# Two-way attention and a rational feed-forward layer on one core: batch 0's attention by token halves, the first weights joined in halves, and a new order of work

## The chip, the cores and the metric

One core of a Trainium2 chip runs the whole kernel in one launch. The metric is the device time in microseconds. A profile records one execution of the program; its span goes from the first to the last instruction.

## The reference

```python
def _attn_ref(x, state):                     # x: 8 x 8 x 512 x 64, state: 8 x 8 x 32 x 64
    scores = scale * np.matmul(x, state.transpose(0, 1, 3, 2))
    scores = scores - scores.max(-1, keepdims=True)
    a = np.exp(scores)
    a /= a.sum(-1, keepdims=True) + 1e-09
    xread = np.matmul(a, state)
    scores2 = scale * np.matmul(state, x.transpose(0, 1, 3, 2))
    ...
    sread = np.matmul(a2, x)
    return np.concatenate([xread, sread], axis=2)

def _moe_ref(x, w_in, w_out, a, b):          # 4608 x 512, 512 x 2048, 2048 x 512
    h = x @ w_in
    P = a[0] + a[1] * h + a[2] * h2 + a[3] * h3
    Q = 1.0 + np.abs(b[0]) * np.abs(h) + np.abs(b[1]) * h2
    g = P / (Q + 1e-06)
    return g @ w_out
```

Tokens read from 32 state slots per head and slots read from 512 tokens per head. The 544 rows of each of 8 batches then go through a layer whose activation is a ratio of two polynomials. The weights arrive as 64-bit numbers.

## The kernel before

**The work.** A unit of work is a pair of a batch `b` and one of eight slices `u` of the 2048 hidden columns, n = 8b + u; 64 units for the tokens, and 8 more (n = 64 to 71) for the slots of all batches together. Instead of `xread` times `w_in` the kernel multiplies the state by the slice of `w_in` first (`extra`, L689, token `X`, 32 small matmuls at L695, for two batches at a time), and the attention weights with that product afterwards (`front`, L762, token `F`, at L785). Both are split in a high and a low float32r part, so each `F` has 6 matmuls, two `F` per unit. The products for later batches go to DRAM (`xs`, L716) and come back (`lm`, L735).

**One unit.** `FC` and `FB` (ScalarE, L794, L801) and `mu`, `po`, `qd` (VectorE, L806, L810, L816) form the polynomials from the PSUM tile `h`; `qa`, `ln`, `ex` (ScalarE, L822, L891, L902) the reciprocal; `g1`, `g2`, `g3` (VectorE, L826, L833, L839) the high part `gh` and the rest; `gl` (GpSimd, L845) the low part; `mh` (4 matmuls) and `ml` (2 matmuls, both at L857) add the product with `w_out` for one 128-token block `t`.

**The weights.** Each slice of `w_in` and `w_out` is a group `g` of raw 64-bit words, 128 x 1024 of them, loaded in two halves of 512 KB (`lr`, L271). `cp` (ScalarE, L293) takes the upper words of one half, `jr` (VectorE, L308) the lower words of the whole group, `jl` (VectorE, L313) joins both to float32. Group 0 is slice 0 of `w_in`, which the first `X` needs. `wh` and `wl` split a `w_out` slice.

**Batch 0's attention** has functions of its own (L507 to L605). `scores0` (L507) takes half of the tokens, from `xT` loads of 512 KB, into two PSUM banks, one for even and one for odd heads (parity `j`). Everything after goes by parity: `sc_copy0` copies one bank (ScalarE), `row_T0` transposes it (TensorE, L528), `row_max0`, `row_sub0` (VectorE), `row_exp0` (ScalarE), `row_sum0` (VectorE) and `row_norm0` (GpSimd) are the softmax over slots; `a_T0` transposes back, `a_hi0` and `a_lo0` (L585, L590) write the two parts of `aT`. `col_max`, `col_scale`, `col_exp` are the softmax over tokens, `e2_T0` and `e2_copy0` its transposes, and `sread` (L607) with `sr_copy`, `sr_T`, `sr_fin` the read by the slots.

**What sets the order.** `ORDER` (L23 to L195) is a string of tokens, one per call, with the arguments behind colons. The program walks it, and each engine executes its own instructions in that order; semaphores are added where one needs another's result. SP issues nearly all DMAs in that order too, so a DMA that waits for a buffer holds up those behind it. The PSUM tiles `h`, `ps_x`, `ps_c`, `ps_sr` share two slots of two banks (tag `h`); the other four banks (tags `o0` to `o3`) hold the output sums, and at the start batch 0's small tiles. The raw weights, and later `lm`, share two buffers, but for groups that borrow the place of a later `wo`. `lc`, `cb`, `cv` load, spread and copy the constants; `b0a` the absolute value of one. `lx` loads the next tile of `xT` or `x` in the order in which the list uses them; `ls` loads the state, `ws` stores a joined slice, `lw` loads it again, `os` stores output.

Of the kernel before, what the change touches and what calls it, by code (L numbers as in the profile page):

```python
# [1028 lines left out]
```

## Time and profile before

| | us |
|---|---|
| median of 3 runs | 674.07 |
| lowest and highest | 673.9, 674.11 |
| the profiled execution, its own time | 675.09 |
| its span | 673.3 |

The profiled execution took 1.79 us more than its span, and 1.02 us more than the median. In the views each engine has its name: PE is TensorE, PEld its weight loads, DVE VectorE, ACT ScalarE, POOL GpSimd, SP the queue that issues DMAs. A `q` behind the name is the engine's sequencer. An arrow in a wait points from the one that waits to the one waited for. Names of tiles stand as out<-in.

### The profile page before, as it was taken

How to read it: one execution, taken by the hardware profiler on the slowest of the kernel's cores; microseconds unless marked ns; L12 is line 12 of the kernel's file. 1: busy time of each engine (PE TensorE's matmuls, PEld its weight loads, DVE VectorE, ACT ScalarE, POOL GpSimd, SP SyncE). 2: the span in 40 equal slices, each digit the busy share in tenths (PEclk: the TensorE clock that was granted, in tenths of full speed). 3: DMA queues.
4: the chain of work that ended last, by engine and by line, in shares of the span. 5: the costliest groups of instructions: out<-in, count | busy, mean ns of one | idle time of the engine just before them, and what ended most of it. 6: DMA issues, size and time to landing. Idle time of an engine off the chain costs nothing.

```text
span 673.3 us, 11301 instructions
## 1 busy us (share of the span) xinstructions
PE 650.9 (97%) x4474; PEld 509.5 (76%) x4474; DVE 629.3 (93%) x583; ACT 521.7 (77%) x633; POOL 307.8 (46%) x174
## 2 busy tenths in 40 slices
PE   4699999999999999999999999999999999999997
PEld 2466667877877777878878878778778788788895
DVE  4999999899999898999999999999999999998886
ACT  4989989887978788878687777877786868777473
POOL 0234446534644545363544355443554444544540
PEclk9979999999999999999999999999999999999999
DMA  8979887343066164044232210412220311203301
GB/s 329 373 253 356 297 285 251 110 142 127 17 180 210 48 215 149 29 134 140 85 107 88 91 48 17 139 49 77 95 79 17 125 33 47 64 31 94 91 21 47
DMA packets 30679, 85.67 MB, mean 127 GB/s; under 512 B 3490, under 2 KB 3618, under 8 KB 30626
## 3 DMA queue, kind: packets, MB, share of 16 engines
q1 hardware_dynamic: 30290, 84.56, 36.9%
q8 instruction: 35, 0.57, 0.4%
q10 hardware_dynamic: 336, 0.39, 0.3%
q14 instruction: 18, 0.15, 0.1%
HBM read 57.15 MB, written 27.79 MB: 126 GB/s over the span
## 4 chain that ended last, share of the span: by engine, by line
PE 41%; DVE 34%; ACT 11%; issue 9%; POOL 2%; DMA 1%; SPq 0%; DVEq 0%; POOLq 0%; ACTq 0%
PE h L785 13%; DVE gh L829 7%; DVE C L808 5%; DVE A L818 5%; DVE A L835 5%; DVE C L812 3%; DVE C L841 3%; PE ps_x L695 2%; POOL gl L848 2%; PE o__5821 L857 2%; PE o__5809 L857 2%; ACT A L824 1%; ACT cv_y L300 1%; ACT C L797 1%; DVE aT L500 1%
## 5 line engine op out<-in xcount | busy, mean ns | idle before, releaser
L848 POOL TENSOR_TENSOR gl<-C,L 128x1024 fp32r<-128x1024 f32 (+1 forms) x70 | 176.0, 2516 | 255.1 <-DVE C L841 164.9
L785 PE MATMUL h<-aT,m 128*128 128x512 f32 x768 | 188.8, 392 | 1.3 <-DVE m L731 0.6
L785 PEld LDWEIGHTS h<-aT,m 128*128 128x128 f32 x768 | 142.5, 188 | 37.2 <-DVE m L731 2.3
L829 DVE SCALAR_TENSOR_TENSOR gh<-C,cst,L 128x1024 fp32r<-128x1024 f32 (+1 forms) x72 | 94.4, 1312 | 12.9 <-ACT L L904 9.9
L797 ACT ACTIVATE C<-h,cst 128x1024 f32<-128x1024 f32 (+1 forms) x72 | 83.3, 1157 | 28.1 <-PE h L785 23.2
L804 ACT ACTIVATE A<-h,cst 128x1024 f32<-128x1024 f32 (+1 forms) x72 | 76.8, 1067 | 32.6 <-PE h L785 26.9
L744 POOL TENSOR_TENSOR m<-m_sb,m 128x512 fp32r<-128x512 f32 x56 | 80.1, 1439 | 36.2 <-ACT m L740 20.4
L835 DVE SCALAR_TENSOR_TENSOR A<-A,gh 128x1024 f32<-128x1024 f32 (+1 forms) x72 | 91.5, 1270 | 1.7
L841 DVE SCALAR_TENSOR_TENSOR C<-C,cst,A 128x1024 f32<-128x1024 f32 (+1 forms) x72 | 89.4, 1246 | 1.4
L824 ACT ACTIVATE A<-A 128x1024 f32<-128x1024 f32 (+1 forms) x72 | 72.9, 1013 | 22.9 <-DVE A L818 22.5
L818 DVE SCALAR_TENSOR_TENSOR A<-A,b0a,h 128x1024 f32<-128x1024 f32 (+1 forms) x72 | 86.9, 1215 | 3.4 <-ACT A L804 2.4
L812 DVE SCALAR_TENSOR_TENSOR C<-C,cst,h 128x1024 f32<-128x1024 f32 (+1 forms) x72 | 87.7, 1219 | 1.9
L808 DVE TENSOR_TENSOR C<-C,h 128x1024 f32<-128x1024 f32 (+1 forms) x72 | 82.9, 1152 | 4.2 <-ACT C L797 3.8
L894 ACT ACTIVATE L<-A 128x1024 f32<-128x1024 f32 (+1 forms) x72 | 73.0, 1014 | 5.2 <-POOL gl L848 1.4
L904 ACT ACTIVATE L<-L 128x1024 f32<-128x1024 f32 (+1 forms) x72 | 72.9, 1013 | 1.8
L695 PE MATMUL ps_x<-win_sb,st 64*32 64x256 f32 x1024 | 37.7, 420 | 2.9 <-DVE win_sb L320 2.2
L740 ACT CAST m<-m_sb 128x512 fp32r<-128x512 f32 x56 | 34.0, 615 | 5.1 <-PE h L785 2.2
L695 PEld LDWEIGHTS ps_x<-win_sb,st 64*32 64x32 f32 x1024 | 18.1, 114 | 18.1 <-issue 7.4
L337 POOL TENSOR_TENSOR wo<-cv_r,wo 128x512 fp32r<-128x512 f32 x16 | 21.7, 1378 | 19.6 <-ACT wo L330 19.6
L785 PEld LDWEIGHTS h<-sh,m 128*128 128x128 f32 x192 | 23.9, 191 | 1.6 <-POOL sh L912 0.6
L785 PE MATMUL h<-sh,m 128*128 128x256 f32 x192 | 24.4, 284 | 0.4 <-POOL sh L912 0.4
L490 POOL TENSOR_TENSOR e<-e,rs 128x512 f32<-128x512 f32 x14 | 16.4, 1189 | 17.6 <-DVE rs L484 13.1
(246 smaller groups left out, 1109.1 us busy)
## 6 DMA issues: line engine op xcount, KB each, us to landing
m_sb<-m_dram SPq DMA_DIRECT2D x56, 256.0 KB, 3.0
xT_sb<-in_xT_dram SPq DMA_DIRECT2D x16, 512.0 KB, 4.4
x_sb<-in_x_dram SPq DMA_DIRECT2D x16, 512.0 KB, 6.9
m_dram<-xo SPq DMA_DIRECT2D x16, 512.0 KB, 4.2
win_sb<-w_in_dram SPq DMA_DIRECT2D x16, 512.0 KB, 5.0
out_dram<-o_sb SPq DMA_DIRECT2D x32, 256.0 KB, 3.7
raw<-in_w_in_dram SPq DMA_DIRECT2D x10, 512.0 KB, 7.5
raw_w<-in_w_out_dram SPq DMA_DIRECT2D x8, 512.0 KB, 7.2
```

Source lines behind the costliest of these rows:

```text
L744: nc.gpsimd.tensor_tensor(m[:, 1], MF.pop(n), m[:, 0].bitcast(F32), op=ALU.subtract)
L785: nc.tensor.matmul(h[:, ci * W : (ci + 1) * W], l, r, start=(q == 0), stop=(q == len(seq) - 1),)
L797: nc.scalar.activation(e["C"], e["h"], AF.Identity, scale=cst[:, 3:4], bias=cst[:, 2:3])
L804: nc.scalar.activation(e["A"], e["h"], AF.Abs, scale=cst[:, 5:6])
L808: nc.vector.tensor_tensor(e["C"], e["C"], e["h"], op=ALU.mult)
L812: nc.vector.scalar_tensor_tensor(e["C"], e["C"], cst[:, 1:2], e["h"], op0=ALU.add, op1=ALU.mult)
L818: nc.vector.scalar_tensor_tensor(e["A"], e["A"], b0a, e["h"], op0=ALU.add, op1=ALU.mult)
L824: nc.scalar.activation(e["A"], e["A"], AF.Abs)
L829: nc.vector.scalar_tensor_tensor(e["gh"], e["C"], cst[:, 0:1], e["L"], op0=ALU.add, op1=ALU.mult)
L835: nc.vector.scalar_tensor_tensor(e["A"], e["A"], 1.0 + 1e-6, e["gh"].bitcast(F32), op0=ALU.add, op1=ALU.mult)
L841: nc.vector.scalar_tensor_tensor(e["C"], e["C"], cst[:, 0:1], e["A"], op0=ALU.add, op1=ALU.subtract)
L848: eng.tensor_tensor(e["gl"], e["C"], e["L"], op=ALU.mult)
```

## The change

Batch 0's scores go into the shared two-bank PSUM tile, and the steps from `sc_copy0` to `a_lo0` take half of the tokens with both parities instead of one parity with all tokens. `scores0` now calls `scores` (L373), which is the same but for the place. `jr` and `jl` take a half as a second argument; without one they work on the whole group as before. `cp`, `front` and `mm` get a form that takes a whole group, or half a unit (numbers from 100 on); no token of the new list uses these forms. The list has the same tokens as before, but for `jr:0` and `jl:0`, which become `jr:0:0`, `jr:0:1`, `jl:0:0` and `jl:0:1`, in another order from the first on; both lists end with `ml:71:0 fl:71:0 os:71:0 ml:70:1 ml:71:1 fv:71:1 os:71:1`. Shown up to `F:2:0`:

```diff
 ORDER = [
-    "lx ls:0:2 lc pre lx scores0:0 scores0:1 sc_copy0:0 sc_copy0:1 row_T0:1 col_max:0 row_T0:0 lr:0:0 "
-    "cp:0:0 lr:0:1 jr:0 cp:0:1 row_max0:0 lr:1:0 ls:2:8 cp:1:0 jl:0 X:1 row_max0:1 row_sub0:1 "
-    "row_exp0:1 X:0 row_sub0:0 row_exp0:0 XA:1 lr:1:1 cp:1:1 lr:3:0 jr:1 X:2 row_sum0:0 row_norm0:0 "
-    "col_scale:0 col_exp:0:0 e2_T0:0 XA:0 fh:0 row_sum0:1 col_exp:0:1 lr:2:0 fo:0 XA:2 a_T0:0 a_hi0:0 "
-    "row_norm0:1 jl:1 a_T0:1 lr:2:1 a_hi0:1 cb cv X:4 lr:4:0 lr:4:1 cp:2:0 cp:2:1 a_lo0:0 lr:3:1 XA:4 "
-    "a_lo0:1 F:0:0 jr:2 F:0:1 jl:2 fh:1 cp:3:0 fo:1 F:1:0 lx F:1:1 lx cp:4:0 b0a jr:3 col_eps:0 "
-    "cp:3:1 jr:4 FB:0 FC:0 jl:3 wh:3 wl:3:0 lr:5:0 wl:3:1 lr:5:1 FB:1 qd:0 qa:0 ln:0 ex:0 mu:0 qd:1 "
-    "po:0 ws:1 e2_T0:1 e2_copy0:0 e2_copy0:1 sread:0:0 sread:0:1 cp:5:0 jr:5 cp:5:1 FC:1 g1:0 qa:1 "
-    "mh:0:2 xs:1 g2:0 col_norm:0 sr_copy:0 g3:0 xs:0 lr:7:0 lr:7:1 ln:1 sr_T:0 sr_fin:0 cp:4:1 ws:0 "
-    "ex:1 mu:1 po:1 X:5 XA:5 gl:0 jl:5 wh:5 wl:5:0 jl:4 lr:8:0 g1:1 X:8 XA:8 fh:2 cp:7:0 cp:7:1 "
-    "mh:0:0 ml:0:0 fo:2 lr:6:0 lr:6:1 xs:5 jr:7 lr:9:0 xs:2 X:9 lr:8:1 g2:1 xs:4 jl:7 wl:5:1 XA:9 "
-    "F:2:0 F:2:1 FC:2 FB:2 X:6 cp:6:0 lr:11:0 g3:1 lr:9:1 mh:0:1 jr:6 XA:6 xs:6 ml:0:1 qd:2 cp:6:1 "
...
+    "ls:0:2 pre lx scores0:0 sc_copy0:0 lr:0:0 cp:0:0 row_T0:0 jr:0:0 jl:0:0 row_max0:0 row_sub0:0 lx "
+    "scores0:1 sc_copy0:1 row_T0:1 row_exp0:0 lr:0:1 cp:0:1 jr:0:1 ls:2:8 col_max:0 jl:0:1 "
+    "col_scale:0 col_exp:0:0 col_exp:0:1 row_max0:1 row_sub0:1 row_exp0:1 row_sum0:0 row_norm0:0 X:1 "
+    "row_sum0:1 lr:1:0 cp:1:0 lr:1:1 jr:1 X:0 XA:1 XA:0 fh:0 fo:0 cp:1:1 jl:1 X:2 a_T0:0 XA:2 lc cb "
+    "cv a_hi0:0 a_lo0:0 row_norm0:1 a_T0:1 a_hi0:1 a_lo0:1 e2_T0:1 lr:2:0 cp:2:0 lr:2:1 b0a jr:2 "
+    "cp:2:1 jl:2 X:4 fh:1 XA:4 lr:4:0 cp:4:0 lr:3:0 cp:3:0 lr:3:1 lr:4:1 cp:3:1 F:0:0 F:0:1 FB:0 fo:1 "
+    "col_eps:0 col_norm:0 F:1:0 F:1:1 lr:5:0 jr:3 jl:3 xs:1 jr:4 FC:0 wh:3 wl:3:0 wl:3:1 FB:1 qd:0 "
+    "qa:0 e2_T0:0 ln:0 ex:0 e2_copy0:0 e2_copy0:1 mu:0 qd:1 cp:5:0 po:0 lr:5:1 jr:5 cp:5:1 xs:0 lx lx "
+    "sread:0:0 g1:0 mh:0:2 ws:0 cp:4:1 qa:1 FC:1 lr:7:0 xs:4 g2:0 sread:0:1 sr_copy:0 mh:0:3 jl:5 "
+    "wh:5 sr_T:0 sr_fin:0 g3:0 ln:1 ex:1 ws:1 mu:1 po:1 lr:7:1 X:5 XA:5 X:8 XA:8 gl:0 ml:0:2 jl:4 "
+    "g1:1 fh:2 lr:6:0 fo:2 cp:7:0 jr:7 cp:6:0 mh:0:1 cp:7:1 lr:6:1 cp:6:1 X:9 F:2:0 g2:1 xs:2 xs:5 "
...
 ]
@@ -291,12 +290,12 @@
             )
 
     def conv_parts(g, k):
-        if k == 0:
+        if k != 1:
             y = cv.tile([P, 4 * CW], I32, name="cv_y", tag="cv")
             r = cv.tile([P, 4 * CW], I32, name="cv_r", tag="cv")
             CV[g] = y, r
         y = CV[g][0]
-        sl = slice(2 * k * CW, (2 * k + 2) * CW)
+        sl = slice(0, 4 * CW) if k == 2 else slice(2 * k * CW, (2 * k + 2) * CW)
         nc.scalar.activation(
             y[:, sl].bitcast(F32),
             RAW[g][:, sl, 1].bitcast(F32),
@@ -305,20 +304,36 @@
             alpha=-(2.0**32),
         )
 
-    def join_rest(g):
+    def words(k):
+        return slice(0, 4 * CW) if k is None else slice(2 * k * CW, (2 * k + 2) * CW)
+
+    def join_rest(g, k=None):
+        sl = words(k)
         nc.vector.tensor_scalar(
-            CV[g][1], RAW[g][:, :, 0], 2.0**-29, 7.0, op0=ALU.mult, op1=ALU.min
-        )
-
-    def join(g):
+            CV[g][1][:, sl],
+            RAW[g][:, sl, 0],
+            2.0**-29,
+            7.0,
+            op0=ALU.mult,
+            op1=ALU.min,
+        )
+
+    def join(g, k=None):
         what, u = groups[g]
         y, r = CV[g]
         w = r
         if what == "in":
-            w = win_t[u] = ld.tile([P, NP, CW], F32, name="win_sb", tag="win", bufs=3)
-            w = w.rearrange("p c f -> p (c f)").bitcast(I32)
+            if not k:
+                win_t[u] = ld.tile([P, NP, CW], F32, name="win_sb", tag="win", bufs=3)
+            w = win_t[u].rearrange("p c f -> p (c f)").bitcast(I32)
+        sl = words(k)
         nc.vector.scalar_tensor_tensor(
-            w, y, 3, r, op0=ALU.logical_shift_left, op1=ALU.bitwise_or
+            w[:, sl],
+            y[:, sl],
+            3,
+            r[:, sl],
+            op0=ALU.logical_shift_left,
+            op1=ALU.bitwise_or,
         )
 
     def store_win(u):
@@ -505,25 +520,16 @@
         return ps_o.tile([P, S], F32, name=name, tag=f"o{t}")
 
     def scores0(g):
-        xt = X.pop(("xT", 0, g))
+        scores(0, g)
+
+    def tokens_of(t, g):
+        return t[:, :, g * (S // 2) : (g + 1) * (S // 2)]
+
+    def sc_copy0(g):
+        T = TS[0]
         if g == 0:
-            TS[0] = {"pj": [obank("ps_sc0", j) for j in range(2)]}
-        w = S // 2
-        for k in range(NP):
-            for j in range(2):
-                nc.tensor.matmul(
-                    TS[0]["pj"][j][k * NS : (k + 1) * NS, g * w : (g + 1) * w],
-                    st[j * D : (j + 1) * D, 0, k, :],
-                    xt[j * D : (j + 1) * D, k, :],
-                    start=True,
-                    stop=True,
-                )
-
-    def sc_copy0(j):
-        T = TS[0]
-        if j == 0:
             T["s"] = at.tile([P, 2, S], F32, name="sT", tag="sT")
-        nc.scalar.copy(T["s"][:, j], T["pj"][j])
+        nc.scalar.copy(tokens_of(T["s"], g), tokens_of(T["ps"], g))
 
     def transposes0(ps, src):
         for t in range(NT):
@@ -531,10 +537,17 @@
                 ps[:, t * P : (t + 1) * P], src[:, t * P : (t + 1) * P], ident
             )
 
-    def row_T0(j):
+    def row_T0(g):
         T = TS[0]
-        T["pr", j] = obank("ps_s0", 2 + j)
-        transposes0(T["pr", j], T["s"][:, j])
+        T["pr", g] = obank("ps_s0", 2 + g)
+        s = tokens_of(T["s"], g)
+        for t in range(NT):
+            j, i = divmod(t, NT // 2)
+            nc.tensor.transpose(
+                T["pr", g][:, t * P : (t + 1) * P],
+                s[:, j, i * P : (i + 1) * P],
+                ident,
+            )
 
     def half(t):
         return t.rearrange("p (a s) -> p a s", s=NS)
```

The parts of `front`, `mm` and `mm_hi` that the list doesn't use are left out here.

## Rows read from the trace of the kernel before

**Rows 1.** The page, part 1: busy us, share of the span, instructions.

```profile
PE 650.9 (97%) x4474; PEld 509.5 (76%) x4474; DVE 629.3 (93%) x583; ACT 521.7 (77%) x633; POOL 307.8 (46%) x174
```

**Rows 2.** Windows: stretch, length, busy PE, PEld, DVE, ACT, POOL, granted clock, DMA share, GB/s.

```profile
14.00:33.00 19.00, 13.94 (x166) 8.92 (x154) 17.58 (x27) 18.64 (x31) 4.60 (x4) 0.99 0.99 390
33.00:45.00 12.00, 11.33 (x172) 6.60 (x173) 11.24 (x11) 10.71 (x17) 5.03 (x3) 0.59 0.62 192
45.00:160.00 115.00, 113.81 (x1041) 83.00 (x1041) 109.50 (x104) 102.21 (x124) 55.38 (x31) 1.00 0.68 235
160.00:640.00 480.00, 477.65 (x2886) 383.51 (x2886) 460.50 (x404) 367.57 (x429) 233.38 (x124) 1.00 0.28 90
...
42.00:43.00 1.00, 1.00 (x3) 0.77 (x4) 0.49 (x1) 1.00 (x3) 0.75 (x1) 0.63 0.91 365
```

**Rows 3.** Waits of TensorE, whole span: us in total, times, longest.

```profile
PE ps_sr L618 <- ACT e2T L605: 4.8, 1, 4.8
PE ps_x L695 <- DVE win_sb L320: 2.2, 2, 1.9
...
PE o__4169 L857 <- POOL gl L848: 0.4, 1, 0.4
```

**Rows 4.** Timeline of TensorE, 0 to 46 us: start, us, engine, line, operation.

```profile
5.17 1.11 PE L514 MATMUL ps_sc<-xT_sb,st 64*32 64x256 f32 x16 [5.17 <-DMA xT_sb<-in_xT_dram]
6.72 1.11 PE L514 MATMUL ps_sc<-xT_sb,st 64*32 64x256 f32 x16 [0.44 <-DMA xT_sb<-in_xT_dram]
...
12.99 5.44 PE L695 MATMUL ps_x<-win_sb,st 64*32 64x256 f32 x96 [1.92 <-DVE win_sb L320]
...
20.66 1.10 PE L695 MATMUL ps_x<-win_sb,st 64*32 64x256 f32 x32 [0.24 <-DVE win_sb L320]
21.68 6.00 PE L785 MATMUL h<-aT,m 128*128 128x512 f32 x24
27.52 0.60 PE L530 MATMUL ps_e<-ident,e 128*128 128x128 f32 x4
32.95 2.21 PE L618 MATMUL ps_sr<-x_sb,e2T 128*32 128x64 f32 x64 [4.83 <-ACT e2T L605]
35.09 2.08 PE L857 MATMUL o__409<-wo,gh 128*128 128x512 f32 x4
...
38.15 3.67 PE L695 MATMUL ps_x<-win_sb,st 64*32 64x256 f32 x64 [0.62 <-ACT srT L641]
...
44.81 1.43 PE L785 MATMUL h<-aT,m 128*128 128x512 f32 x5
```

**Rows 5.** Timeline of ScalarE, 0 to 46 us.

```profile
7.92 1.07 ACT L526 COPY sT<-ps_sc 128x512 f32<-128x512 f32 x2 [5.46 <-PE ps_sc L514]
...
14.29 1.23 ACT L566 ACTIVATE e<-e 128x512 f32<-128x512 f32 x2 [2.79 <-DVE e L560]
...
25.11 1.15 ACT L804 ACTIVATE A<-h,cst 128x1024 f32<-128x1024 f32 x1
...
32.33 1.05 ACT L605 COPY e2T<-ps_e 128x512 f32<-128x512 f32 x2
```

**Rows 6.** Timeline of VectorE, 0 to 46 us.

```profile
9.02 1.22 DVE L398 TENSOR_REDUCE cm<-sT 128x2 f32<-128x1024 f32 x1 [9.02 <-ACT sT L526]
...
11.72 1.22 DVE L320 SCALAR_TENSOR_TENSOR win_sb<-cv_y,cv_r 128x1024 int32<-128x1024 int32 x1
...
41.22 1.27 DVE L829 SCALAR_TENSOR_TENSOR gh<-C,cst,L 128x1024 fp32r<-128x1024 f32 x1
```

**Rows 7.** VectorE by line and shape: count, busy us, mean ns, idle before.

```profile
L808 DVE TENSOR_TENSOR C<-C,h 128x1024 f32<-128x1024 f32 x64 | 77.5, 1211 | 2.0 <-ACT C L797 1.6 <-issue 0.4
...
L731 DVE TENSOR_TENSOR m<-ps_x,m 128x512 fp32r<-128x512 f32 x8 | 5.5, 682 | 1.1 <-ACT m L727 1.1
```

**Rows 8.** The tile `x_sb`, 10 to 40 us: from issue to landing.

```profile
DMA to landing us min/median/max: 11.1/11.3/11.5
```

**Rows 9.** The page, part 5: the group of `gl`.

```profile
L848 POOL TENSOR_TENSOR gl<-C,L 128x1024 fp32r<-128x1024 f32 (+1 forms) x70 | 176.0, 2516 | 255.1 <-DVE C L841 164.9
```

More of the change, by code (lines that the diff above doesn't have):

```diff
@@ L583, in a_T0, with by_parity @@
         transposes0(T["pa", j], T["e1"][:, j])
+    def by_parity(t):
+        return t.rearrange("p (j t) -> p j t", j=2)
     def a_hi0(j):
@@ L587, in a_hi0 @@
             AT[0] = at.tile([P, 2, 2, S], F32R, name="aT", tag="aT", bufs=2)
-        nc.scalar.copy(AT[0][:, 0, j], TS[0]["pa", j])
+        nc.scalar.copy(tokens_of(AT[0][:, 0], j), by_parity(TS[0]["pa", j]))
     def a_lo0(j):
@@ L592, in a_lo0 @@
         nc.vector.tensor_tensor(
-            a[:, 1, j], TS[0]["pa", j], a[:, 0, j].bitcast(F32), op=ALU.subtract
+            tokens_of(a[:, 1], j),
+            by_parity(TS[0]["pa", j]),
+            tokens_of(a[:, 0], j).bitcast(F32),
+            op=ALU.subtract,
         )
@@ L760, in attention_rational_ffn, with unit, of_half @@
     EW, SRS, O, OS = {}, {}, {}, {}
-    def front(n, ci):
-        b = n // U
-        if b < B:
+    HALVES = 100
+    def unit(n):
+        return n if n < HALVES else (n - HALVES) // 2
+    def of_half(n):
+        return None if n < HALVES else (n - HALVES) % 2
+    def front(n, ci):
+        half = of_half(n)
+        b = unit(n) // U
+        if half is not None:
+            W = S // 2
+            cols = slice(half * W, (half + 1) * W)
+            rhs = [(AT[b][:, 0, j, cols], AT[b][:, 1, j, cols]) for j in range(2)]
+        elif b < B:
             rhs = [(AT[b][:, 0, j, :], AT[b][:, 1, j, :]) for j in range(2)]
@@ L770, in front @@
             W = B * NS
-        if ci == 0:
+        if ci == 0 and half != 1:
             h = ps_h.tile([P, 2, S], F32, name="h", tag="h")
-            h = h.rearrange("p f w -> p (f w)")[:, : 2 * W]
-            EW[n] = {"h": h, "W": W, "N": 2 * W}
+            EW[n] = {"h": h.rearrange("p f w -> p (f w)")[:, : 2 * W], "W": W, "N": 2 * W}
+            if half == 0:
+                EW[n + 1] = {"h": h[:, 1], "W": W, "N": 2 * W}
         h = EW[n]["h"]
         hh, hl, lh = [], [], []
-        for (m, g), (rh, rl) in zip(M[n], rhs):
+        for (m, g), (rh, rl) in zip(M[unit(n)], rhs):
             mh = m[:, 0, g, ci * P : (ci + 1) * P]
@@ L850, in mm @@
     def mm(n, t, parts):
-        u = n % U
+        u = unit(n) % U
         e = EW[n]
         W = e["W"]
+        x = t * P % W
         for j in range(2):
@@ L858, in mm @@
                     O[t],
-                    e[l][:, j * W + t * P : j * W + (t + 1) * P],
+                    e[l][:, j * W + x : j * W + x + P],
                     WO[u][:, j, k, :],
@@ L865, in mm_hi @@
     def mm_hi(n, t):
-        if n % U == 0:
+        if unit(n) % U == 0:
             O[t] = ps_o.tile([P, DM], F32, name=f"o{t}_", tag=f"o{t}")
```

318 rows, old and new, of the table ORDER are left out of this document.

## Prediction, made before the changed kernel ran

> **What bounds the kernel now.** I read the page first, then the windows, TensorE's waits, and the first 46 us of the timeline one engine at a time.
>
> The page shows TensorE (PE) busy 650.9 of 673.3 us [rows 1]. The windows say where the rest lies: from 45 to 640 us it idles 1.19 and then 2.35 us, so 19 of the 22.4 idle microseconds lie in the first 45 us and in the tail [rows 2]. In that middle VectorE (DVE) is busy too, 109.5 of 115 us and then 460.5 of 480. So the steady part is bound by TensorE with VectorE right behind it, and a change can earn only what the start loses, plus what waits are left in the middle.
>
> TensorE's list of waits puts its two largest waits on another engine into the start: 4.8 us for the copies of `e2T` on ScalarE (ACT) and 2.2 us for the first joined weights [rows 3]. On its timeline [rows 4] the scores begin at 5.17, the first `X` (L695) at 12.99, the first `F` (L785) at 21.68, `sread` at 32.95 after a hole since 28.1, and the next `F` at 44.81. The engine also runs slowly there: 96 matmuls of L695 take 5.44 us from 12.99, 57 ns each, and 32 of them 1.10 us from 20.66, 34 ns each; 64 of them take 3.67 us from 38.15. The granted clock of 33 to 45 us is 0.59, a mixture of the two levels 1.2 and 2.4 GHz [rows 2]. The mean of 14 to 33 us is 0.99 and that of 42 to 43 us 0.63 [rows 2], so the clock fell at the end of the hole and rose again near 42.7.
>
> ScalarE stands 2.79 us waiting for VectorE's subtraction up to 14.29, and from there to the copies at 32.33 it is filled without a gap worth the name [rows 5] (18.64 of 19 us from 14 to 33 [rows 2]). So the hole ends when ScalarE has worked through its queue, and that queue starts when VectorE has finished the first softmax steps.
>
> **Part one: halves at the start.** The first half of group 0's weights now stands in the DMA queue between the two halves of `xT`, and 512 KB take 1.55 us there (the two scores start at 5.17 and 6.72 [rows 4]). So the first scores start as before, the second ones one transfer later, at about 8.3. Scores 1.1 and a copy of half of 1.07 [rows 5] bring the second `sc_copy0` to 9.95. On VectorE `col_max:0` (1.22 [rows 6]) follows to 11.15, then only the second half of the join, about 0.65, instead of the 1.22 at 11.72 behind a `row_max0`. The first half of `jr`, `jl`, `row_max0` and `row_sub0` fits in ahead of 9.95, where VectorE was idle until 9.02. `X:1` starts at 11.9, 1.1 us earlier than 12.99.
>
> Splitting costs something: a 128x512 operation takes 682 ns where a 128x1024 one takes 1211 [rows 7], so two halves cost 0.15 us more each for `jr` and `jl`. The first halves are hidden under the wait for `xT`; without that cover it would be 0.3 us. The copies in token halves read two pieces of 256 instead of one of 512; no row has that shape, I bound it by 0 and 0.1 us each and take 0.
>
> **Part two: ScalarE's queue.** Its steady stretch starts at 12.0 (`col_exp`, which needs `col_scale` at 11.9) instead of 14.29, with as much left to do: one `row_exp0` is done already, `cp:1:0` is not yet. Before, that work took 25.11-14.29 = 10.8 us, up to `FB:0` [rows 5]. That would give 22.8. But `X:1`, `X:0` and `X:2` still run at 57 ns a matmul, 1.8 us each, so `XA:2` waits for `X:2` until 17.3, `cv` for the spread of the constants until 18.5, and `fh:1` for `X:4` until 20.7: 0.95 us in all. `FB:0` starts at 23.75, 1.35 us earlier (bounds: 2.3 without those waits, 0 if they grow to that size). From `FB:0` to `e2_copy0` the same eight steps follow, 32.33-25.11 = 7.2 us [rows 5], so `sread:0:0` starts at 31.6 instead of 32.95.
>
> Its `x` tiles are now issued behind `xs:1`, `lr:5:1` and `xs:0` in SP's queue; `lr:5:0` ahead of them waits for `jr:1` and `cp:1:1`, until 17. They took 11.1 to 11.5 us from issue to landing [rows 8]; issued at 18 to 19 they land by 30. If that cover is gone, each microsecond past 31.6 costs one, for `mh:0:2` and all else on TensorE stand behind it.
>
> **Part three: from sread to the second F.** Before, 11.86 us lie between 32.95 and 44.81, almost all at the low level: `sread` 2.21, `mh:0:2` 2.08, 64 of `X` 3.67 [rows 4]. Now `sread` is cut in two and `mh:0:2`, `mh:0:3` are put between, so that TensorE has hardly a hole from 31.6 to 38. ScalarE and VectorE set bounds to the gain. On VectorE `jr:4` ends at 25.9; `qd`, `mu`, `qd`, `po` at 1.24 each, `jr:5` 0.65 and `g1:0` 1.27 [rows 6] end at 32.8, and `g2`, `jl:5`, `g3`, `mu:1`, `po:1` at 39.0. On ScalarE the copies end at 31.9; three `cp` of 0.6, `qa` 1.1, `FC` 1.2, `sr_copy` 0.5, `wh:5` 0.95 and `sr_fin` 0.3 end at 37.75. If the clock stays up or returns by about 36, TensorE meets these bounds: `X:5` starts at 37.8, `X:8` behind `po:1` at 39.05; `ln:1`, `ex:1`, `XA:5`, `XA:8`, `fh:2` end at 41.7, `fo:2` (0.7) at 42.4, and `F:2` starts at 42.6. If it stays low until 42.7 as before, the two halves of `sread` (1.1 each) and two `mh` (2.08 each [rows 4]) end at 38.05, for `g1:0` holds the first `mh` until 32.85; `sr_T` and `sr_fin` take until 38.95, both `X` 3.67 to 42.6, then `ml`, `mh` and `X:9` 2.5, and `F:2` starts at 45.2. I take 43.4, nearer to the early end: before, the rise near 42.7 came after TensorE had run almost unbroken since 38.15, and now the unbroken stretch begins at 31.6. Ahead of `F:2` one `mh` more is done than before, four matmuls, 0.9 us at the high level. TensorE's lead is 44.81-43.4+0.9 = 2.3 us.
>
> The Trainium skill ("TensorE: Matmul & The Clock Gate", HAM oscillation) says that a long idle pause throttles the array again, so that the next burst starts cold. The trace agrees, with its fall in the hole that ends at 32.95; by that rule alone the new hole, from 27.3 to 31.6, brings the fall back, and the sum would be that of the second rival.
>
> **Part four: the rest of the list.** All later work is the same in another order. What it can win is bounded by the idle time of TensorE from 45 to 640 us, 3.5 us [rows 2]; I bound the loss by as much and take 0. Both lists end with the same seven tokens.
>
> **Sum.** The profiled execution took 675.09 us for its span of 673.3. Less 2.3 that is 672.8. The median of the runs is 674.07, 1.02 lower, which gives 671.8.
>
> **The rivals.**
> - *The clock does not fall at all.* For: the hole is 0.5 us shorter. Against: it is still 4.3 us long. Then `F:2` starts at 42.6, the lead is 3.1 and the time 671.0.
> - *The clock stays low as long as before.* For: the hole. `F:2` at 45.2 with 0.9 us of work done ahead is a lead of 0.5: 673.6.
> - *VectorE takes the lead away.* `g1:1` starts at 41.22 [rows 6]; now it comes behind `po:1` and `jl:4`, at 40.2, only 1.0 us earlier, for `jr:4` stands ahead of `qd:0` in the new order. With 109.5 of 115 us busy, VectorE can give back only some of TensorE's lead. Then 1.0 us remains: 673.1. Against it: TensorE's idle share of the middle is smaller than VectorE's. The Trainium skill ("Perfetto Trace Analysis", Identifying the Most-Contended Engine) says that matmul busy time is no good measure and weight loads are the better one; those are busy 76% here, under VectorE's 93% [rows 1]. By that, this rival would be the likeliest; the trace cannot decide it.
> - *Slower: the new list meets GpSimd's products late.* An output matmul stands in order on TensorE, and a `gl` (L848) takes 2.5 us, 70 times [rows 9]; before, the longest wait on one in the middle is 0.4 us [rows 3]. If the new order has `ml` ahead of its `gl` four times by 1 us in the 600 us, 4.0 us are lost against 2.3 won: 675.8. It decides from 2.3 us of such waits on.
>
> **How the numbers follow.** About 0.2% (1.35 us) is what a measurement of this kernel can tell from no change, so faster means below 672.7. Forecast 0.40 (own range 670.8 to 673.0, 0.37 of it faster), clock stays up 0.15 (faster), clock low as long 0.17 (same), VectorE 0.16 (0.04 faster, 0.12 same), slower 0.12. That makes faster 0.37+0.15+0.04, and 0.02 for a middle that gains by itself, 0.58; same 0.30; slower 0.12. The range goes from 669.7 (the fast rival with a good microsecond of the middle's waits gone) to 674.8, which leaves out most of the slower case.
>
> **What would show it.** In the profile after: first `X` (L695) at 11.9, first `F` (L785) at 20.7 instead of 21.68, first `FB` (L804 before) at 23.75, `sread` at 31.6, a granted clock of 33 to 45 us above 0.59, `F:2` near 43.4; and from 45 us on TensorE idling no more than 3.5 us up to 640. A first `X` at 13 or later would say that the third transfer or the split join is late; a `sread` that waits for a DMA would say that the `x` tiles were the price; waits of `o` for `gl` above 2 us in sum would speak for the slower rival.

## The result, and the profile after

The changed kernel takes **664.14 us** (median of four runs, 663.78 to 664.94) against 673.99 for the kernel before, run beside it: ratio 0.9858 [0.9841, 0.9875], 9.9 us less. The forecast was 671.8 with a range of 669.7 to 674.8, so the direction was right and the size was not: 7.7 us of the gain were not foreseen. The profiled execution took 664.94 us with a span of 663.1, 10.15 us under the one of before.

Of the page after: busy time of each engine, as in [rows 1], and of part 4 (the chain that ended last) the shares by engine.

```profile
PE 643.5 (97%) x4474; PEld 508.5 (77%) x4474; DVE 624.8 (94%) x585; ACT 521.5 (79%) x633; POOL 313.5 (47%) x174
...
PE 87%; DVE 6%; issue 3%; DMA 2%; ACT 2%; POOL 0%; SPq 0%; DVEq 0%; POOLq 0%; ACTq 0%
```

The same line of part 4 for the kernel before:

```profile
PE 41%; DVE 34%; ACT 11%; issue 9%; POOL 2%; DMA 1%; SPq 0%; DVEq 0%; POOLq 0%; ACTq 0%
```

TensorE is busy 97% of the span in both, and VectorE 93 and 94%. By these shares nothing has changed. The chain says otherwise: before, it went through VectorE for a third of the time; now it is TensorE nearly throughout.

Windows of after (columns as in [rows 2]): the start, the middle as in [rows 2], and 45 to 595 us, in which no unit from 64 on has its `F` yet (the first of these smaller matmuls comes at 598.22 us here, at 608.12 before), so that `F`, `mh` and `ml` consist of equal matmuls. Below it the same stretch of the kernel after in a second execution, on another chip ("once more" in the experiments), and of the kernel before.

```profile
31.00:34.00 3.00, 2.95 (x36) 1.80 (x31) 2.96 (x3) 3.00 (x6) 0.00 (x0) 0.50 1.01 380
34.00:35.00 1.00, 1.00 (x34) 0.79 (x34) 1.00 (x2) 1.00 (x2) 0.00 (x0) 1.00 1.03 410
33.00:45.00 12.00, 10.78 (x155) 6.70 (x155) 11.38 (x11) 10.74 (x16) 6.84 (x3) 0.96 0.70 255
45.00:160.00 115.00, 113.99 (x1045) 83.28 (x1044) 112.34 (x105) 101.15 (x122) 59.28 (x32) 1.00 0.68 234
160.00:640.00 480.00, 479.67 (x2931) 389.98 (x2930) 459.88 (x413) 374.60 (x439) 236.89 (x125) 1.00 0.27 88
45.00:595.00 550.00, 548.65 (x3708) 433.32 (x3707) 533.27 (x472) 444.31 (x519) 271.40 (x143) 1.00 0.36 120
```

```profile
45.00:595.00 550.00, 549.30 (x3713) 434.52 (x3712) 532.90 (x473) 444.91 (x519) 272.38 (x143) 1.00 0.35 121
```

```profile
45.00:595.00 550.00, 546.88 (x3684) 427.79 (x3684) 530.84 (x467) 441.04 (x516) 267.20 (x142) 1.00 0.36 122
```

**The column to read is the count behind PE.** From 45 to 595 us TensorE executes 3708 matmuls instead of 3684, 24 more, while its busy time grows by 1.77 us only. The second execution of the same kernel has 3713, so counts a few apart say nothing. The small matmuls (`X`, scores, `sread`) are equally many in this stretch, so the 24 are matmuls of `F`, `mh` and `ml`, which follow each other every 0.23 us (four of L890 start at 655.92 in the timeline of after, the next four at 656.83). So some 5.5 us more of work got done in the same time, and 3.7 us of them were lost before inside what the page calls busy.

The timeline of TensorE after, 0 to 46 us and the three rows just used, as in [rows 4] (L396 is the scores, L714 `X`, L817 `F`, L637 `sread`, L890 `mh` and `ml`):

```profile
4.76 1.11 PE L396 MATMUL ps_sc<-xT_sb,st 64*32 64x256 f32 x16 [4.76 <-DMA st<-in_stT_dram]
...
8.43 1.11 PE L396 MATMUL ps_sc<-xT_sb,st 64*32 64x256 f32 x16 [0.64 <-DMA xT_sb<-in_xT_dram]
...
11.33 3.39 PE L714 MATMUL ps_x<-win_sb,st 64*32 64x256 f32 x64
...
19.86 5.81 PE L817 MATMUL h<-aT,m 128*128 128x512 f32 x24
...
30.82 1.35 PE L637 MATMUL ps_sr<-x_sb,e2T 128*32 128x64 f32 x32 [4.71 <-ACT e2T L624]
32.10 2.05 PE L890 MATMUL o__393<-wo,gh 128*128 128x512 f32 x4
34.08 0.65 PE L637 MATMUL ps_sr<-x_sb,e2T 128*32 128x64 f32 x32
34.67 1.20 PE L890 MATMUL o__426<-wo,gh 128*128 128x512 f32 x4
...
42.01 3.01 PE L817 MATMUL h<-aT,m 128*128 128x512 f32 x12 [0.27 <-DVE m L750]
...
598.22 1.96 PE L817 MATMUL h<-sh,m 128*128 128x256 f32 x15
...
655.92 1.07 PE L890 MATMUL o__5820<-wo,gh 128*128 128x512 f32 x4
656.83 1.10 PE L890 MATMUL o__5820<-wo,gl 128*128 128x512 f32 x4
```

The start did what the prediction said, somewhat better: `F:2` begins at 42.01 instead of 44.81 [rows 4], with one `mh` (0.9 us) more done ahead of it. That is a lead of 3.7 us between these two executions; a good part of it is the clock's and not the change's, as the experiments show. The spans differ by 10.2, so the other 6.5 us were won behind it, where the prediction had put 0.

**How time hides in a busy engine.** Three places of the kernel before, first on TensorE's timeline, then on that of its weight loads:

```profile
56.88 0.73 PE L857 MATMUL o__571<-wo,gl 128*128 128x512 f32 x2
58.20 2.11 PE L785 MATMUL h<-aT,m 128*128 128x512 f32 x8 [0.59 <-DVE m L731]
...
431.64 1.07 PE L857 MATMUL o__4169<-wo,gh 128*128 128x512 f32 x4
433.06 0.73 PE L857 MATMUL o__4169<-wo,gl 128*128 128x512 f32 x2 [0.35 <-POOL gl L848]
...
525.88 0.61 PE L857 MATMUL o__4754<-wo,gl 128*128 128x512 f32 x2
526.99 1.20 PE L857 MATMUL o__4731<-wo,gh 128*128 128x512 f32 x4 [0.50 <-DVE gh L829]
```

```profile
58.20 1.92 PEld L785 LDWEIGHTS h<-aT,m 128*128 128x128 f32 x9 [1.03 <-DVE m L731]
...
433.06 0.30 PEld L857 LDWEIGHTS o__4169<-wo,gl 128*128 128x128 f32 x2 [0.78 <-POOL gl L848]
...
526.99 0.76 PEld L857 LDWEIGHTS o__4731<-wo,gh 128*128 128x128 f32 x4 [0.92 <-DVE gh L829]
```

Four matmuls from 431.64 are over for the next one after 0.91 us, at 432.55; it starts at 433.06, 0.51 later, of which the row shows 0.35. At 526.99 it is 0.66, of which 0.50 show, and at 58.20 it is 0.87, of which 0.59 show, for there a short stall lies between the two matmuls ahead too. The 0.16 between is the modelled end of the pipelined matmul, so a stall under some 0.16 us shows no idle time at all. Of the steps from a matmul of `F`, `mh` or `ml` to the next one, those that are over 0.1 us longer than the usual 0.227 lose 11.2 us in 68 places of the kernel before from 45 to 640 us, and 5.8 us in 46 of the one after (4.3 in 39 in its second execution). TensorE's idle time is 3.5 and 1.3 us there.

### The profile page after: what moved, and what is told of

It reads as the page before. It is cut to its first block, busy times and chain, and to the rows that moved or that the text cites. A ratio compares the mean times of both kernels' runs of the same rounds, so it can differ in the third digit from the quotient of the medians.

```text
span 663.1 us, 11300 instructions
## 1 busy us (share of the span) xinstructions
PE 643.5 (97%) x4474; PEld 508.5 (77%) x4474; DVE 624.8 (94%) x585; ACT 521.5 (79%) x633; POOL 313.5 (47%) x174
## 4 chain that ended last, share of the span: by engine, by line
PE 87%; DVE 6%; issue 3%; DMA 2%; ACT 2%; POOL 0%; SPq 0%; DVEq 0%; POOLq 0%; ACTq 0%
PE h L817 28%; PE ps_x L714 3%; PE o__2202 L890 2%; PE o__4162 L890 2%; PE o__4153 L890 2%; PE o__2245 L890 2%; PE o__2194 L890 2%; PE o__4771 L890 2%; PE o__3564 L890 2%; PE o__2263 L890 2%; PE o__3531 L890 2%; PE o__5313 L890 2%; PE o__5820 L890 2%; PE o__5815 L890 2%; PE o__4766 L890 2%
## 5 line engine op out<-in xcount | busy, mean ns | idle before, releaser
L817 PE MATMUL h<-aT,m 128*128 128x512 f32 x768 | 186.4, 391 | 0.8 <-DVE m L750 0.6
L817 PEld LDWEIGHTS h<-aT,m 128*128 128x128 f32 x768 | 143.3, 188 | 34.0 <-DVE m L750 1.7
L861 DVE SCALAR_TENSOR_TENSOR gh<-C,cst,L 128x1024 fp32r<-128x1024 f32 (+1 forms) x72 | 97.4, 1353 | 10.1 <-ACT L L937 8.2
L763 POOL TENSOR_TENSOR m<-m_sb,m 128x512 fp32r<-128x512 f32 x56 | 81.8, 1470 | 38.1 <-ACT m L759 34.5
L867 DVE SCALAR_TENSOR_TENSOR A<-A,gh 128x1024 f32<-128x1024 f32 (+1 forms) x72 | 85.8, 1192 | 1.5
L714 PE MATMUL ps_x<-win_sb,st 64*32 64x256 f32 x1024 | 35.5, 389 | 2.7 <-ACT xo_w L732 1.1
L714 PEld LDWEIGHTS ps_x<-win_sb,st 64*32 64x32 f32 x1024 | 17.3, 108 | 17.6 <-issue 5.1
L352 POOL TENSOR_TENSOR wo<-cv_r,wo 128x512 fp32r<-128x512 f32 x16 | 23.5, 1486 | 14.8 <-ACT wo L345 8.7
L817 PEld LDWEIGHTS h<-sh,m 128*128 128x128 f32 x192 | 24.1, 191 | 0.6
L732 ACT COPY xo<-ps_x 128x1024 f32<-128x1024 f32 (+1 forms) x24 | 20.8, 873 | 4.5 <-PE ps_x L714 4.3
L817 PE MATMUL h<-sh,m 128*128 128x256 f32 x192 | 24.3, 283 | 0.0
```

Of the source, the lines that this page charges most:

```text
L763: nc.gpsimd.tensor_tensor(m[:, 1], MF.pop(n), m[:, 0].bitcast(F32), op=ALU.subtract)
L817: nc.tensor.matmul(h[:, ci * W : (ci + 1) * W], l, r, start=(q == 0), stop=(q == len(seq) - 1),)
L861: nc.vector.scalar_tensor_tensor(e["gh"], e["C"], cst[:, 0:1], e["L"], op0=ALU.add, op1=ALU.mult)
L867: nc.vector.scalar_tensor_tensor(e["A"], e["A"], 1.0 + 1e-6, e["gh"].bitcast(F32), op0=ALU.add, op1=ALU.mult)
```

## The experiments

Sixteen kernels ran; each time is a median, and its ratio is to the kernel before on the same chip (673.92 to 674.38 us). The theory after the result, A in the expectations, was that the start gave its 3.7 us and that the new order of the rest saves TensorE short stalls for late operands, some 6 us. Rivals were that one of the two gave all, and that the old middle was paced by VectorE (B in the expectation of the first mending, V later).

### Start and rest apart

One list up to `F:2:0`, and the remaining tokens in the order of the other. The third kernel has the new functions and the old list.

```diff
-ORDER = after
+ORDER = after[:after.index("F:2:0")] + [rest in the order of before]     # e1, functions of after
+ORDER = before[:before.index("F:2:0")] + [rest in the order of after]    # e2, functions of before
+ORDER = before, with jr:0 and jl:0 in halves                             # e6, functions of after
```

> The changed kernel's list up to its first F:2:0, then all other tokens in the order of the kernel before (jr:0 and jl:0 in halves, as they stand in the new start). Theory A, start and middle add up: the start alone gives what TensorE was ahead at F:2, 2.8 us earlier (42.01 against 44.81) and one mh (0.9 us) more, so 3.5 to 3.7 us, 670.3 to 670.5. Theory B, the middle of the old order takes the lead away because VectorE binds there: about 673, with F:2 still at 42.0 and the lead gone by 200 us. Theory C, all 9.9 us come from the start, since a lead once won lets the old middle run without its waits: 664 to 666.

> The kernel before with its own start up to F:2:0, its own functions, and then all other tokens in the new order. Theory A: the start as before (first X at 13.0, sread at 33.0, F:2 at 44.8), the rest saves what is left of the 9.9 us, about 6.2 us: 667.5 to 668.0, and TensorE idles about 1.4 us from 45 to 640 instead of 3.5. Theory B: the old start costs little, since the new middle is what counts: 664 to 666. Theory C: 672 to 674.

> The changed functions (batch 0 by token halves, jr and jl of group 0 in halves, one right behind the other) under the list of the kernel before. All theories: no step can start earlier by this, since both scores stand ahead of the first copy. VectorE pays for the split of jr and jl (0.43 and 0.69 for a half against 0.68 and 1.22 for the whole in the two traces, so 0.2 and 0.15 more), and the first join comes 0.35 later: 673.9 to 674.5. If it is 1 us or more faster, the new functions and not the order bring a part of the gain.

| | us | ratio | matmuls, 45 to 595 us |
|---|---|---|---|
| new start, old rest | 672.46 | 0.998 [0.9971, 0.9989] | 3679 |
| old start, new rest | 667.75 | 0.9908 [0.9892, 0.9923] | 3703 |
| old list, new functions | 674.43 | 1.001 [1.0, 1.0019] | 3681 |

The functions alone win nothing. **The new rest alone wins 6.2 us, with the old start**, as theory A had it; that the start gave all is excluded. But the start alone wins 1.5 us, at 672.46, nearer to the rival's 673 than to the 670.3 to 670.5 of theory A: this number of it fell. At the seam TensorE waits 1.0 us for a `gl`, and the old rest executes no more matmuls in its stretch than before. The two gains sum to 7.7, not 9.9; where the other 2.2 come from is not shown. The intervals of the three ratios reach 0.6 to 1.1 us to either side, so it may be a good deal less.

The 3.7 us that theory A counted on were in good part the clock's. Three kernels of the sections below (the old list mended by hand, with less on VectorE, with GpSimd lighter) leave everything up to `F:2` as it is in the kernel before. First the window from 38 to 42 us of the kernel before and of these three, then their `F:2` (that of before is in [rows 4]):

```profile
38.00:42.00 4.00, 3.85 (x65) 1.80 (x66) 4.00 (x4) 3.40 (x5) 1.08 (x1) 0.50 0.71 240
38.00:42.00 4.00, 4.00 (x94) 2.36 (x88) 4.00 (x4) 4.00 (x7) 1.52 (x2) 1.00 0.81 281
38.00:42.00 4.00, 3.71 (x78) 2.23 (x86) 4.00 (x4) 4.00 (x8) 1.53 (x2) 1.00 0.75 256
38.00:42.00 4.00, 4.00 (x93) 2.38 (x101) 4.00 (x4) 4.00 (x6) 1.54 (x2) 1.00 0.77 266
...
42.92 3.01 PE L784 MATMUL h<-aT,m 128*128 128x512 f32 x12 [0.46 <-DVE m L730]
43.38 3.01 PE L778 MATMUL h<-aT,m 128*128 128x512 f32 x12 [0.46 <-DVE m L724]
43.04 3.01 PE L782 MATMUL h<-aT,m 128*128 128x512 f32 x12 [0.45 <-DVE m L731]
```

The granted clock of the kernel before is 0.50 there, that of the three is back at 1.00, and their `F:2` begins at 42.92 to 43.38 instead of 44.81. The kernel after varies too. In its second execution the clock is still at 0.50 from 34 to 37 us, where the first had 1.00 from 34 on, and `F:2` begins at 42.39:

```profile
34.00:37.00 3.00, 3.00 (x37) 2.23 (x37) 2.96 (x4) 2.48 (x4) 1.35 (x1) 0.50 0.91 347
...
42.39 3.02 PE L817 MATMUL h<-aT,m 128*128 128x512 f32 x12
```

The chips differ as well, but on one and the same chip the old list with less on VectorE has `F:2` at 43.38, and that with more on VectorE, its start as unchanged, has the clock low until 42.0 and `F:2` at 44.34. So the time at which the clock returns differs between executions of the same work, and 3.7 us compares a late return with an early one. Against the three, the two executions of after are 1.4 to 2.3 us ahead, with the one `mh`; the 1.5 us of the new start alone agree with that.

### The terms of the start

`sread` in one piece again, with the `mh` behind the second `X`; and the first group's low bits and join whole again.

```diff
-"sread:0:0 g1:0 mh:0:2 ... sread:0:1 sr_copy:0 mh:0:3 ... X:8 XA:8"
+"sread:0:0 sread:0:1 g1:0 mh:0:2 ... sr_copy:0 ... X:8 mh:0:3 XA:8"      # e3
-"... jr:0:0 jl:0:0 ... jr:0:1 ... col_max:0 jl:0:1"
+"... jr:0 ... col_max:0 jl:0"                                            # e4
```

> The changed kernel with both halves of sread again together ahead of mh:0:2, and mh:0:3 behind X:8, as in the order of before; nothing else moved. If the fill between 31 and 36 us is what brought TensorE's clock back early (granted 1.00 from 34 us instead of from 42.7), the clock now stays low longer, with a mean of 33 to 45 us of 0.6 to 0.8 instead of 0.96, F:2 starts 1 to 2 us later and the time is 665 to 666. Rival: the clock comes back at the same place whatever stands there; then F:2 and the time move by less than 0.5 us, 664.0 to 664.6.

> The kernel after with the first group's join whole again: one copy of the low bits and one join of 128x1024 in the places of their second halves, the two loads and converts still in halves. VectorE then has 1.9 us ahead of col_max instead of the 1.1 us of the second halves, so the first X starts 0.7 to 0.9 us later, at 12.0 to 12.2. If the start sets the end (theory A): 664.5 to 665.2 us. If ScalarE's queue hides it: 664.0 to 664.4.

> The kernel after once more, on the chip of the three runs beside it: 663.8 to 664.9 us by all theories; it gives the small differences of the others a base on the same chip.

Measured: 665.01 us for `sread` together (0.9863 [0.9846, 0.9879]), 664.85 for the whole join (0.9861 [0.9846, 0.9876]), 664.39 for the kernel after once more (0.9851 [0.9837, 0.9866]). Both come out about half a microsecond slower, inside the intervals, so no cost is shown for either. With `sread` together the mean clock of 33 to 45 us is 0.79 and `F:2` begins at 44.19, close to what the first theory expected. But the kernel after once more, with nothing undone, has 0.82 and 42.39, and since the clock returns at different times by itself, one execution can't say that the fill brings it back. The traces show more of the join. With the whole join the first `X` starts at 12.86, 1.5 us later than after's 11.33, twice the expected shift:

```profile
12.86 1.53 PE L714 MATMUL ps_x<-win_sb,st 64*32 64x256 f32 x24 [1.35 <-DVE win_sb L330]
```

In the kernel after, the second half of the join runs from 11.39 to 12.07 on VectorE, so its `X` at 11.33 had begun **before** that half was there: the first eight of its matmuls start by 11.77 and read only the first half, the next one starts at 12.13. The split join gives this too, not only a shorter wait.

### Mending TensorE's order by hand

If the stalls are an affair of where TensorE's tokens stand, they can be mended in the old list. Twenty tokens, six `mh` (four matmuls) and fourteen `ml` (two), went ahead of the 17 largest stalls; likewise ten in the new list. Two of the moves:

```diff
-"... XA:10 ml:1:1 lr:10:0 F:3:0 F:3:1 FC:3 X:16 ... FB:3 XA:16 mh:1:1 ..."
+"... XA:10 ml:1:1 lr:10:0 mh:1:1 F:3:0 F:3:1 FC:3 X:16 ... FB:3 XA:16 ..."
-"... qa:42 mh:40:0 ft:44 ml:41:0 ... ln:42 ex:42 ml:40:1 ..."
+"... qa:42 mh:40:0 ft:44 ml:40:1 ml:40:0 ml:41:0 ... ln:42 ex:42 ..."
```

> The kernel before with its own list, in which 20 output-matmul tokens (mh, ml; four matmuls each, about 0.9 us of TensorE) are moved ahead of 17 places where TensorE stood a while inside its busy time in the trace of before; these 17 places lose 8.27 us in sum there. Nothing else changes, the start included. Theory A (short stalls of TensorE in the old order, waits for gh, gl, m and the rest that the weight loads show, are what the middle loses): most of the 8.27 us comes back, less what the moved work meets later: 666.5 to 669.5 us against 674.0. Rival B (VectorE is the bound of the old order and the stalls are only its shadow): the stalls go to other places and the time stays at 673.0 to 674.5. In the trace A expects less than 6 us of stalls from 45 to 640 us (before: 11.3), B as many as before.

> The kernel after with ten mh and ml tokens moved ahead of the eight largest stalls that are left in it from 45 us on, 2.4 us in sum. Theory A: 1 to 2 us less than the kernel after, 662.0 to 663.3 us. If the rest of the new order is already bound by TensorE's matmuls or by VectorE there, no change: 663.8 to 664.6.

Measured: **675.35 us** in the old list, 1.0018 [1.0008, 1.0027], a little slower; 664.45 in the new one, 0.9857 [0.9842, 0.9872], no change to 664.39. Theory A in this form falls. The 17 places are mended in the trace, but the stalls came back elsewhere, 12.2 us in 70 places by the count above, and TensorE executes 3677 matmuls from 45 to 595 us instead of 3684. The weight loads' waits for `gl` and `gh` grew from 7.5 us, 17 times, to 11.2 us, 22 times (after: 4.1 us, 14 times), for example

```profile
PEld o__490 L856 <- POOL gl L847: 1.4, 1, 1.4
...
PEld o__2945 L856 <- POOL gl L847: 1.0, 2, 0.8
```

An output matmul that is moved ahead is missing later, when TensorE again has nothing whose operand is there. This speaks for V; other moves might have fared better, so it excludes this mending, not every one.

### VectorE's load

`row_max` and `row_sub` of batches 1 to 7 left out (17.2 us less for VectorE), and `row_max` three times (17.0 us more), in either list.

```diff
 def row_max(b):
     T["mx"] = at.tile([P, NT * 8], F32, name="mx", tag="mx", bufs=2)
     nc.vector.tensor_reduce(T["mx"], slots(T["e1"]), axis=AX.X, op=ALU.max)
+    nc.vector.tensor_reduce(T["mx"], slots(T["e1"]), axis=AX.X, op=ALU.max)
+    nc.vector.tensor_reduce(T["mx"], slots(T["e1"]), axis=AX.X, op=ALU.max)
```

> The kernel before with less work on VectorE: row_max and row_sub of batches 1 to 7 are left out (the row softmax is then taken without its maximum), 1.22 + 1.24 us in seven places, 17.2 us in sum from 45 us on. TensorE's work and order stay. Theory V (in the old list VectorE's pace sets the middle as much as TensorE's matmuls do; the short stalls of TensorE are its shadow): the time falls by 5 to 9 us, to 665 to 669, where TensorE's own work takes over. Theory A (TensorE's order against late operands, whatever VectorE's pace): at most 1.5 us, 672.5 to 674.

> The kernel after with the same 17.2 us of VectorE's work left out. If the new list is bound by TensorE (its chain is 87% TensorE): at most 2 us less, 662 to 664.4. If VectorE still has a share in the bound as in the old list: 658 to 660.

> The kernel before with row_max of batches 1 to 7 issued three times instead of once, 2.43 us more for VectorE in seven places, 17.0 us in sum, nothing else changed. Theory V: VectorE has no slack in the old list, nearly all of it shows: 686 to 692. Theory A: VectorE's 25 idle microseconds of the middle take a good part of it: 676 to 684.

> The kernel after with the same 17.0 us more on VectorE. If the new list keeps VectorE ahead of TensorE by some slack, a part of it is hidden: 668 to 678, that is 4 to 13 us more, less than the same edit costs the old list. If the slack is nil: 680 to 682.

| | less on VectorE | more on VectorE |
|---|---|---|
| old list | 671.45, 0.9961 [0.9946, 0.9976] | 695.65, 1.032 [1.0297, 1.0343] |
| new list | 665.37, 0.9877 [0.9861, 0.9894] | 683.26, 1.0132 [1.0116, 1.0147] |

More work costs the old list 21.7 us and the new one 18.9, in both more than the 17.0 added, and what I expected of the new one (4 to 13 us) was wrong. **Neither list hides much of a burst of 2.4 us on VectorE.** Part of what goes beyond the 17.0 can be seen in the traces: TensorE's clock fell again, twice in the new list and once in the old, after stretches with long pauses (in the new list TensorE was busy 3.21 and 2.23 us of the 5 ahead of these two windows):

```profile
105.00:108.00 3.00, 2.91 (x7) 2.33 (x8) 2.96 (x4) 2.91 (x6) 3.00 (x4) 0.50 0.72 258
317.00:320.00 3.00, 3.00 (x9) 2.33 (x8) 2.93 (x4) 2.51 (x3) 0.21 (x1) 0.50 0.02 5
```

With less work the old list wins 2.5 us, more than A and less than V allowed; the new list wins nothing. The relief was smaller than planned, for other operations took longer: VectorE's busy time fell by 11.0 us in the old list (629.3 to 618.3) and by 9.7 in the new (624.8 to 615.1), not by 17.2. So VectorE holds up the old middle, but is a part of it only.

### All three helpers

Relief for GpSimd (no `split_lo`, 80 us less), for ScalarE (no `quad_abs` in every fourth unit), and all three together, with the same in the new list.

```diff
 def split_lo(n):
-    m = M[n][0][0]
-    nc.gpsimd.tensor_tensor(
-        m[:, 1], MF.pop(n), m[:, 0].bitcast(F32), op=ALU.subtract
-    )
+    MF.pop(n)
 def front(n, ci):
-            ml = m[:, 1, g, ci * P : (ci + 1) * P]
+            ml = m[:, int(not U <= n < B * U), g, ci * P : (ci + 1) * P]
 def quad_abs(n):
-    nc.scalar.activation(e["A"], e["A"], AF.Abs)
+    if n % 4:
+        nc.scalar.activation(e["A"], e["A"], AF.Abs)
```

> The kernel before without GpSimd's 56 splits of the reloaded weights (ft, 1.44 us each, 80 us in sum; the front of groups 8 to 63 reads the high part in place of the low one, with as many matmuls). VectorE is then free of their company (6 us of its long operations lie beside a split) and the products gl no longer queue behind them. If GpSimd's products and its collisions with VectorE set the old middle: 4 to 7 us less, 667 to 670. If not: less than 1.5 us, 672.5 to 674.2.

> The kernel before without quad_abs on ScalarE in every fourth group, 1.06 us in 18 places, 17 to 19 us in sum, in the chain of each of these groups. If ScalarE's queue sets the old middle: 4 to 7 us less, 667 to 670. If not: less than 1.5 us, 672.5 to 674.2. VectorE's 17.2 us gave 2.5.

> The kernel before with all three reliefs: GpSimd without its splits, ScalarE without every fourth quad_abs, VectorE without row_max and row_sub of batches 1 to 7. Theory M (in the old list the engines wait for each other in turn, so that no single relief pays): together they give what the new order of the rest gave, 5 to 7 us, 667 to 669. Theory A (the order of TensorE's own tokens is what loses): 670 to 672, no more than the largest single one.

> The kernel after with the same three reliefs. Its middle is TensorE's own work already, so at most 2 us less: 662.5 to 664.5. More than 4 us less would say that the new list too still waits for the others.

| | us | ratio | matmuls, 45 to 595 us |
|---|---|---|---|
| old list, GpSimd lighter | 671.59 | 0.9962 [0.9947, 0.9977] | 3691 |
| old list, ScalarE lighter | 673.61 | 0.999 [0.9981, 0.9999] | 3682 |
| old list, all three | 668.72 | 0.9923 [0.9907, 0.994] | 3704 |
| new list, all three | 664.15 | 0.9851 [0.9836, 0.9866] | 3715 |

No single relief reaches the 4 to 7 us that would make its engine the cause: against 674.38 GpSimd's gives 2.8 and ScalarE's 0.8, and VectorE's gave 2.5. **Together they give the old list 5.7 us, and the new list 0.2.** That is the time of theory M in the expectations, and not that of A. But the three single gains sum to 6.1 us: the reliefs add up, each worth a fraction, and M's premise, that no single relief pays, did not hold. The chain of the old list with all three, part 4 of its page:

```profile
PE 73%; DVE 13%; ACT 7%; issue 4%; DMA 2%; POOL 1%; SPq 0%; POOLq 0%; DVEq 0%; ACTq 0%
```

It is largely TensorE's chain again, and the count of 3704 is that of the old start with the new rest (3703). With lighter helpers, the old order of TensorE's tokens comes within 1 us of the new rest behind the same start (668.72, 667.75). The waits of the weight loads say the same. Summed by the engine waited for, from 45 to 640 us, they are 8.5 us for VectorE, 5.5 for GpSimd and 4.1 for ScalarE in the kernel before, 6.0, 2.1 and 3.2 in the kernel after, and 5.2, 3.9 and 2.9 in the old list with all three reliefs. So the old order lost time in waits for all three engines, and the new order shortens the waits for all three with the same operations. That this is the whole of its gain is argued, not shown: a list with the new order for the helpers alone, or for TensorE alone, did not run.

GpSimd's share has a visible form. VectorE and GpSimd in the kernel before (one timeline each):

```profile
181.32 1.39 DVE L829 SCALAR_TENSOR_TENSOR gh<-C,cst,L 128x1024 fp32r<-128x1024 f32 x1
182.75 2.21 DVE L835 SCALAR_TENSOR_TENSOR A<-A,gh 128x1024 f32<-128x1024 f32 x1
```

```profile
181.58 2.30 POOL L744 TENSOR_TENSOR m<-m_sb,m 128x512 fp32r<-128x512 f32 x1
```

The second operation takes 2.21 us while a split runs beside it until 183.88. The group's means, by line and shape, for the kernel before, after, and the old list without splits:

```profile
L835 DVE SCALAR_TENSOR_TENSOR A<-A,gh 128x1024 f32<-128x1024 f32 x64 | 84.8, 1326 | 1.6
```

```profile
L867 DVE SCALAR_TENSOR_TENSOR A<-A,gh 128x1024 f32<-128x1024 f32 x64 | 80.3, 1255 | 1.3
```

```profile
L832 DVE SCALAR_TENSOR_TENSOR A<-A,gh 128x1024 f32<-128x1024 f32 x64 | 80.8, 1263 | 1.6
```

The new order loses 4.5 us less in this group than the old, with the splits still there: 7 of the 64 operations run beside a split in the kernel before, 3 in the one after. The page of after has VectorE at 624.8 us instead of 629.3 [rows 1] for the same work.

## Why the prediction was wrong

**The step that failed is part four**: the rest of the list "as 0", its gain "bounded by the idle time of TensorE from 45 to 640 us, 3.5 us". It gave 6.5 us in the profiles, 6.2 by itself with the old start. The bound was no bound: the idle time of [rows 2] is what is left after each matmul's modelled end, and the kernel before lost 3.7 us more than the one after from 45 to 595 us inside busy time. The chain of waits stood on the page with VectorE at 34% and was not used; it said that the middle was not TensorE's own. In the two profiles the rest of the miss is the start, 3.7 us instead of 2.3: 1.4 and 6.5, less 0.2 between profiles and medians, are the 7.7. Run by itself the start gives 1.5 us, less than the 2.3, and 2.2 us come only with both, which stays unexplained.

The Trainium skill ("Perfetto Trace Analysis", Identifying the Most-Contended Engine) calls matmul busy time a bad measure because matmuls are pipelined. The runs agree: 97% in both kernels, 9.9 us apart. The weight loads' share, one of the two measures that it names in its place, moved from 76 to 77%. The count of equal matmuls in a stretch and the waits on the weight loads' row told more.

**Part one, halves at the start: right.** Second scores at 8.43 (forecast 8.3), first `X` at 11.33 (11.9), because its first matmuls need only half of the join, which I had not seen.

**Part two, ScalarE's queue: right.** First `F` at 19.86 (20.7; the third group of `X` took 1.10 us, where the sum had 1.8), `FB:0` at 22.99 (23.75), `sread` at 30.82 (31.6); 7.2 us from `FB:0` to the copies as in [rows 5]. Its wait of 4.71 us is for the copies of `e2T`, so the `x` tiles were hidden.

**Part three, the clock: near in the number, by luck.** The clock fell once more in the hole before `sread` and was back by 34 us (0.50 from 31 to 34, 1.00 from 34 to 35), where it had stayed low until near 42.7 [rows 2]. I took 43.4 for `F:2`, with 42.6 if the clock was back by 36; it was, `sread` came 0.8 us earlier, and 42.01 was measured. But the reason given, the unbroken stretch from `sread` on, is not borne out: with the old start unchanged the clock was back before 38 us in three kernels, and in the second execution of the kernel after it was low until past 37. The 2.3 us were reckoned from a profile with a late return, of an execution 1.02 us above the median. That the change moves the clock is not shown.

**The rivals.** The clock did fall, and did not stay low as long; that decides less than the prediction thought, since it varies by itself. "VectorE takes the lead away" describes the kernel that was not built: new start and old rest keep 1.5 us, at 672.46, against the 673.1 forecast for it; in the kernel after the gain was kept. That VectorE is what took the lead there is not shown. The slower rival, output matmuls that meet `gl` late, did not happen in the new list: the weight loads wait 2.1 us for `gl` from 45 to 640 us, 4.3 before. The hand-mended old list ran into it, with 7.7.

**What stays open** is which of the moved tokens bring the operands in time. Neither is it shown where the 2.2 us come from that only both parts give. The orders differ nearly everywhere, and fewer collisions of VectorE with GpSimd are one visible part, not all.

## What to carry to other kernels

A busy share of 97% says nothing about the last 2%: count the matmuls that a stretch gets done (of one size, and in two executions), look at the weight loads' waits, and take the shares of the chain as a warning when a second engine has a third of it. Where several engines run close to their limits in fixed orders, as here, a stall on one can be a delay handed on by the others: moving work on the waiting engine moved the stalls, relieving one engine returned a fraction, three together about the sum of theirs, and a new order for all engines as much without any relief. When a change reorders the entire list, the reordering is a term of its own, and visible idle time is no bound for it. A lead read from two profiles contains what the clock did in these two executions; look at a second one before it goes into a sum.
